# Windowed attention feeding a gated feed-forward layer: keys and queries brought straight into the score layout, head pairs scored together, partial first sums, and paced casts

## The chip, the cores and the metric

One core of one Trainium2 chip. The metric is the device time of one execution in microseconds (us); a profiled execution also has a span, the time between its first and last instruction, which lies about 1.7 us below the time. All inputs are fp32 in DRAM; the kernel computes in bf16 with fp32 sums.

## The reference, cut to what matters

```python
# q, k, v: (8 batches, 8 heads, 576 rows, 64)
scores = q @ k.transpose(0, 1, 3, 2) / sqrt(64)
rel = pos[:, None] - pos[None, :]
mask_plain = (rel >= 0) & (rel < 32)                       # heads 0-3
mask_dil   = (rel >= 0) & (rel < 128) & (rel % 4 == 0)     # heads 4-7
attn = softmax(where(mask, scores, -1e9)) @ v              # -> x: (4608, 512)
h = x @ w_in                                               # (512, 2048)
out = (h * sigmoid(beta * h)) @ w_out                      # (2048, 512)
```

Nearly all arithmetic is the two products: 9 tiles of 512 rows, each with 64 matmuls of 512 columns for `w_in` and 64 for `w_out`. The attention of batch b + 1 runs in between, as fill.

Of the kernel before, what the change touches and what calls it, by code (L numbers as in the profile page):

```python
# [22 lines left out]
class Op:  # L23
    def __init__(self, engs, fn, deps, vt, acquire, group, dma, lat):
        self.engs, self.fn, self.vt, self.acquire = engs, fn, vt, acquire
        self.deps = [d for d in deps if d is not None]
        self.dma, self.lat, self.group = dma, lat, group
        self.end = self.ready = None
        self.waits = 0
        self.next = []  # L30
        for g in group if isinstance(group, list) else [] if group is None else [group]:
            g.users.append(self)


class Plan:
# [3 lines left out]
    CAPS = {"h": 3, "o": 2, "z": 4, "a": 8, "s": 5}  # L39
# [6 lines left out]
    def op(self, engs, fn, deps=(), vt=0.0, acquire=None, group=None, dma=0, lat=None):  # L46
        acquire = acquire if acquire is None or isinstance(acquire, list) else [acquire]
        o = Op(engs, fn, deps, vt, acquire, group or acquire, dma, lat)
        self.ops.append(o)
        return o  # L50

    def run(self, filler=None, filler_until=0.0):
# [13 lines left out]
        ends = []  # L66

# [19 lines left out]
        while n_left:  # L87
            best = None
            near = {}
            for o in avail:  # L90
                base = o.ready
                at = {e: max([free[e], base] + [t for x, t in o.group.read.items() if x != e]
                             if o.group is not None and e != "PE" else [free[e], base]) for e, d in o.engs}
                fin = min(at[e] + d for e, d in o.engs)
# [18 lines left out]
            if filler is not None and s <= filler_until and free["PE"] + 300 < s:  # L113
# [5 lines left out]
                free["PE"] = now + 225  # L119
                continue  # L120
# [6 lines left out]
            o.fn(e)  # L127
            free[e] = s + d
            o.start, o.end = s, s + d + self.LAT[e]
# [27 lines left out]
FIRST = "KD0 QD0 KD1 QD1 KP0 QP0 KP1 QP1 S2 S3 T S00 S10 V20 V21 V30 V31 U V00 V10 X2 X3 X00 X10 S01 S11 V01 V11 X01 X11"  # L157
LATER = "S2 S3 T V20 V21 V30 V31 U S00 S10 S01 S11 X2 X3 V00 V10 X00 X10 S02 S12 V01 V11 X01 X11"
# [3 lines left out]
def kernel(  # L162
# [35 lines left out]
    ADDED = 1  # L198
    BY_DMA = 2
    SPLIT = 4  # L200
# [16 lines left out]
    def copy(e, out, in_):  # L217
# [10 lines left out]
    mask_e = {n: const([P, 2, 2, 2, QT // 2], BF16, f"maske_{n}") for n in ("FP", "PP")}  # L228
# [5 lines left out]
    warm = const([P, 1], FP32, "warm")  # L234

# [7 lines left out]
    ptt = const([P, 2, 288], BF16, "ptt")  # L243
    ptt_own = ptt[0:2 * KTL][:, :, 0:256].rearrange(
        "p c (h s) -> p c h s", h=4)[:, :, :, 0:2 * UT]
# [9 lines left out]
    raw = const([P, 2, 4, S // 2], BF16, "raw")  # L255
    vd16 = raw[:].rearrange("p z h m -> p (z h m)")[:, 0:1024].rearrange("p (h T d) -> p h T d", h=4, T=C)
    vd16_of = [vd16] * DIRECT + [st[b % 2][:, 0:1024].rearrange(
        "p (h T d) -> p h T d", h=4, T=C) for b in range(DIRECT, B)]
    kT = [const([P, WIN + S], BF16, f"kT{x}") for x in range(2)]
    kz = const([P, 4, WIN + S], BF16, "kz")  # L260
    qd = const([P, 4, 2, S // 2], BF16, "qd")
    qT = qd[:].rearrange("p (x f) e m -> p x (f e m)", x=2)[:, :, 0:S]
# [27 lines left out]
    def t_fill1(e):  # L290
        for x in range(2):
            nc.vector.memset(kT[x][:, 0:WIN], 0.0)
            nc.vector.memset(qt[x][:], 0.0)
# [60 lines left out]
    def t_late(e):  # L354
        band(mask_d[:], [[0, 4]], [(1, P)], 0, WIN - 1, 1.0, 0.0)
        for n in ("PP", "FP"):
            band(mask_e[n][:].rearrange("p a b e m -> p (a b) e m"), [[0, 4]], [(1, 2), (2, QT // 2)],
                 WIN, -1, 1.0, 0.0)
            band(mask_n[n][:].rearrange("p a b n -> p (a b) n"), [[0, 4]], [(1, QT)], WIN, -1, 1.0, 0.0)
        nc.gpsimd.memset(mask_e["FP"][0:WIN, 0], 0.0)  # L360
        nc.gpsimd.memset(mask_n["FP"][0:WIN, 0], 0.0)
        nc.gpsimd.memset(kz[:], 0.0)  # L362
    late_fill = plan.op([("POOL", 11500)], t_late, vt=-.3)


# [15 lines left out]
    def plain_v(b, p0, c0):  # L381
        return bass.AP(tensor=v.tensor, offset=v[b, 0].offset + (p0 - WIN) * D + c0 * QT * D,
                       ap=[[D, (P if not p0 else P - WIN) if not c0 else WIN], [QT * D, 4 * NI - c0], [1, D]])

    def direct_vp(b, deps, vt):
        if b:
            return [load("POOL", (vp[b % 2][:, :, 0:D], plain_v(b, 0, 0)), deps, vt, 768, .27, 1450,
                         1100 if b < DIRECT else 4000)]
        return [load("POOL", (vp[0][WIN:P, :, 0:D], plain_v(0, WIN, 0)), deps, vt, 576, .25),
                load("POOL", (vp[0][0:WIN, 1:, 0:D], plain_v(0, 0, 1)), deps, vt, 184, .25)]  # L390

    def direct_vd(b, deps, vt, tdeps=()):
        src = v[b, 4:8].rearrange("h (t T) d -> t h (T d)", T=C)[0:P]
        out = [load("POOL", (vd16_of[b].rearrange("p h T d -> p h (T d)"), src), deps, vt, 512, .35)]
        for c in range(2):
            src = bass.AP(tensor=v.tensor, offset=v[b, 4].offset + ((P - WIN) * C + c) * D,
                          ap=[[2 * D, 2 * KTL], [S * D, 4], [1, D]])
            out.append(load("POOL", (vt_[b % 2][:, c, :, 0:D], src), list(tdeps), vt + (.15 if b == 0 else .02 if b < DIRECT else 0) + .001 + .001 * c, 96, .2))
# [4 lines left out]
    def cast(b, z, deps, vt):  # L403
        dst = scratch[b, z] = dram_pool.tile([2, S * 4 * D], BF16, name=f"s{b}_{z}")
        src = (k, q)[z][b].rearrange("(x h) s d -> x (h s d)", x=2)
        return load("POOL", (dst[:].rearrange("x (a e) -> (x a) e", e=1024),
                             src.rearrange("x (a e) -> (x a) e", e=1024)), deps, vt, 1152, .38)

    def crossbar(b, z, h0, deps, vt):
        flat = scratch[b, z][h0 // 4]  # L410
        if h0:
            dst = (dk, dq)[z][b % 2][:].rearrange("p r h t -> p r (h t)")
            src = flat.rearrange("(a e) -> a e", e=C * D)
        else:
            dst = raw[:, z].rearrange("p h m -> p (h m)").unsqueeze(1)
            src = flat.rearrange("(a e) -> a e", e=P)
# [31 lines left out]
    xcopy = {}  # L448

    def back_dma(b, j, vt_of, vdone):  # L450

        rows = dram_pool.tile([S // 2, HD], BF16, name=f"x{b}_{j}")
        plain = rows[:, 0:HD // 2].rearrange("(i m e) c -> e m i c", e=2, m=QT // 2)
        out = []
        if b < DIRECT:
            out.append(plan.op(
                [("SP", 500)], lambda e: nc.sync.dma_start(
                    out=rows[:, 0:HD // 2].rearrange("(i m) c -> m i c", m=QT),
                    in_=xsp[j][:].rearrange("p a x h d -> p a (x h d)")),
                [vdone[0, j], vdone[1, j]], vt_of[f"X1{j}"], dma=1200, lat=2000))  # L460
        for e_ in range(2 if b >= DIRECT else 0):
            out.append(plan.op(
                [("SP", 500)], lambda e, e_=e_: nc.sync.dma_start(
                    out=plain[e_], in_=xsp[j][e_ * QT // 2:(e_ + 1) * QT // 2].rearrange("p a x h d -> p a (x h d)")),
                [vdone[0, j], vdone[1, j]], vt_of[f"X1{j}"], dma=600, lat=2000))
# [7 lines left out]
        if j:  # L473
            for c in range(C):
                dil.append(plan.op(
                    [("SP", 500)], lambda e, c=c: nc.sync.dma_start(
                        out=right[t1 - t0:, c], in_=xdt[(c % 2 * 2 + c // 2) * UT:(c % 2 * 2 + c // 2 + 1) * UT].rearrange("p x h d -> p (x h d)")),
                    [vdone["U"]], vt_of["X11"], dma=150, lat=2000))
# [13 lines left out]
        for x in range(4):  # L492
            xcopy[b, x, j] = o

    def attention(b, ld, names, vts):
# [4 lines left out]
        if b < DIRECT:  # L500
            for n in [x for x in names if x[0] in "KQ"]:
# [8 lines left out]
                def evac(e, g=g, z=z, kind=kind, i=i):  # L510
                    tp = bank(g, BF16)[:, 0:S]
                    if kind == "P":
                        dst = qT[:, i] if z else kT[i][:, WIN:]
# [4 lines left out]
                key = (("kT", "qT")[z], i) if kind == "P" else (("dk", "dq")[z], kv, i)  # L518
                steps[n] = [plan.op([dve(S), act(S)], evac, [tr, fill1] + war(key), vt, group=g)]
                wrote(key)  # L520
        else:
            vt = vt_of["zPRE"]
            ready = {"D": [ld["x", 0, 4], ld["x", 1, 4]]}
            ops = []
            for e_ in range(2):
                def spread(e, e_=e_):
                    rows = slice(64 * e_, 64 * e_ + 64)
                    dst = kz[rows, :, WIN:].rearrange("p h (m e) -> p h m e", e=2)[:, :, :, e_]
                    copy(e, dst, raw[rows, 0])
                o = plan.op([("POOL", 1200), ("DVE", 1400)], spread, [ld["x", 0, 0], late_fill] + war("kz"), vt)  # L530
                used(("raw", 0), o)
                ops.append(o)
            wrote("kz")
            w = war("qd", ("qT", 0), ("qT", 1))
            for e_ in range(2):
                for half in range(2):
                    def spread(e, e_=e_, half=half):
                        copy(e, qd[64 * half:64 * half + 64, :, e_], raw[64 * e_:64 * e_ + 64, 1])
                    o = plan.op([("DVE", 900)] + ([("POOL", 1150)] if half == e_ else []), spread,
                                [ld["x", 1, 0]] + w, vt)  # L540
                    used(("raw", 1), o)
                    ops.append(o)
            wrote("qd", ("qT", 0), ("qT", 1))
            ready["P"] = ops


        def mixed(e):
            copy(e, dkt[kv][:], dk[kv][:, :, :, CT - KTL:].rearrange("p r h k -> p h k r"))
        o = plan.op([("DVE", 450), ("POOL", 500)], mixed,
                    (steps["KD0"] + steps["KD1"] if b < DIRECT else ready["D"][0:1]) + war(("dkt", kv)), vt_of["T"] - .01)  # L550
# [4 lines left out]
        for c in range(2):  # L555
            def padded(e, c=c):
# [3 lines left out]
            o = plan.op([("DVE", 250), ("POOL", 300)], padded,  # L560
                        (steps["QD0"] + steps["QD1"] if b < DIRECT else ready["D"][1:]) + [fill1] + war(("qt", kv)),
                        vt_of["T"] - .01)
# [8 lines left out]
        vdeps["P"] = ld["vp"] + [(fill3, fill4)[kv]]  # L571
        def spread(e):
            copy(e, vd[kv][:, :, :, 0:D], vd16_of[b])
        o = plan.op([("POOL", 1100), ("DVE", 620)], spread,
                    [ld["vd"][0], (fill3, fill4)[kv]] + war(("vd", kv)), vt)
# [7 lines left out]
        def exp_and_mask(key, sop, g, vt, n, sc, w, m, tiles):  # L583
# [4 lines left out]
            if b >= ADDED or key == ("T",):  # L588
                def mask(e):
                    E[e].tensor_tensor(out=w(), in0=w(), in1=m(), op=ALU.mult)  # L590
                ex = plan.op([("POOL", 120 + 2.2 * n), ("DVE", 160 + .65 * n)], mask,
# [410 lines left out]
```

## The kernel before: the parts that the change and the argument touch

The kernel states operations with a wished position in the stream, and a planner of its own orders them on each engine at build time. So an edit of one wish moves other instructions as well. Four parts matter. From batch 3 on, K and Q of all eight heads are cast to bf16 in two DRAM-to-DRAM copies and transposed by the DMA crossbar (a DMA that transposes what it moves). Those of the dilated heads land in `dk` and `dq` ready for use; those of the plain heads land in `raw` and are spread by VectorE and GpSimd into full-height tiles padded with zero heads:

```python
# two casts per batch, released by the first gated tile of batch b - 2
cs = [cast(b, z, gop[b - 2, 0] + behind, b - 2 + .01 * z) for z in range(2)]
...
dst = kz[rows, :, WIN:].rearrange("p h (m e) -> p h m e", e=2)[:, :, :, e_]
copy(e, dst, raw[rows, 0])                      # spread of K, two copies per batch
...
copy(e, qd[64 * half:64 * half + 64, :, e_], raw[64 * e_:64 * e_ + 64, 1])   # Q, four
```

The plain scores of those batches then run over all 128 rows of the array, one head per matmul:

```python
nc.tensor.matmul(sc[:, a, h2 * QT:h2 * QT + QT],
                 lhsT=kz[:, 2 * x + h2, i * QT:i * QT + P],
                 rhs=qd[:, 2 * x + h2, :, i * QT // 2:(i + 1) * QT // 2], start=True, stop=True)
```

A first-product group waits for all of `xT` of its columns; the first four blocks of tile 0 are cut into column halves. The last block of the output is two halves of 256 columns, whose last half is evicted (copied from the accumulator banks to SBUF) in two pieces:

```python
for lo, hi in ((0, HD // 2), (HD // 2, HD)) if last_one else ((0, HD),):
    block_cols(t, tb, vts, lo, hi, (lo, (lo + hi) // 2, hi) if lo else (lo, hi))
```

The softmax here doesn't subtract the row's maximum and nothing guards it: scores larger than these inputs give would overflow.

## Time and profile before

| kernel before | |
|---|---|
| time, median of 3 | 311.83 us (311.3 to 311.83) |
| span of the profiled run, granted clock | 309.7 us, 0.998 |
| TensorE busy | 96% |
| first `w_in` product starts | 20.07 us |
| last product ends | 305.06 us |
| from there to the end | 4.65 us |

The granted clock is the share of the full TensorE clock that the chip allowed. The lines that bound the kernel are shown in the prediction.

### The profile page before, as it was taken

The page shows a single profiled execution, that of the slowest core. Times are in us where ns is not written, and L with a number is a line of the kernel's source. Part 1 is how long each engine was busy: PE and PEld are TensorE (multiplying, and loading weights), DVE is VectorE, ACT ScalarE, POOL GpSimd, SP SyncE. Part 2 cuts the span into 40 slices and gives each one's busy share as a digit, 9 for nine tenths or more (in the row PEclk, how much of TensorE's full clock was granted, in tenths as well). Part 3 has the DMA queues.
Part 4 walks back from the last instruction along what each step waited for, and adds up shares of the span by engine and source line. Part 5 has one row for each costly group of instructions (what it writes and reads, how often), then busy time and mean ns, then how long its engine had stood idle before and what let it go on. Part 6 is the DMA issues. An engine that isn't in the chain of part 4 may idle for free.

```text
span 309.7 us, 6029 instructions
## 1 busy us (share of the span) xinstructions
PE 297.0 (96%) x2270; PEld 153.6 (50%) x2307; DVE 199.1 (64%) x421; ACT 171.3 (55%) x302; POOL 108.6 (35%) x150
## 2 busy tenths in 40 slices
PE   7899999999999999999999999999999999999994
PEld 5565546454454445444455454445544444444452
DVE  4687868888958777775896878677853443434300
ACT  2668845866448445753775547555754544554311
POOL 8989754537170146414823651154000000000000
PEclk9999999999999999999999999999999999999999
DMA  6999999999689982999999759997024100001112
GB/s 100 168 210 207 206 187 208 230 155 174 155 163 178 191 151 83 180 160 181 188 206 181 197 117 177 129 224 163 18 64 112 44 34 34 36 34 60 42 70 69
DMA packets 93561, 42.48 MB, mean 137 GB/s; under 512 B 71052, under 2 KB 88220, under 8 KB 93212
## 3 DMA queue, kind: packets, MB, share of 16 engines
q0 software_dynamic: 42336, 19.66, 50.3%
q1 hardware_dynamic: 51052, 22.37, 35.0%
q8 instruction: 18, 0.29, 0.4%
q14 instruction: 11, 0.09, 0.1%
q10 hardware_dynamic: 144, 0.07, 0.1%
HBM read 39.32 MB, written 18.87 MB: 188 GB/s over the span
## 4 chain that ended last, share of the span: by engine, by line
PE 82%; POOL 6%; DMA 6%; DVE 2%; issue 2%; ACT 0%; POOLq 0%; ACTq 0%; DVEq 0%
PE bank L856 38%; PE bank L824 35%; DMA raw<-in_v_dram 3%; DMA vp<-in_v_dram 3%; PE bank L703 2%; PE bank L755 2%; POOL st L368 1%; PE bank L740 1%; PE bank L644 1%; PE bank L725 1%; POOL kz L362 1%; DVE qt L218 1%; DVE g L836 1%; PE bank L434 0%; PE bank L618 0%
## 5 line engine op out<-in xcount | busy, mean ns | idle before, releaser
L831 ACT ACTIVATE tnh<-bank,beta_half 128x512 bf16<-128x512 f32 (+2 forms) x148 | 100.1, 677 | 81.8 <-PE bank L824 73.6
L836 DVE SCALAR_TENSOR_TENSOR g<-tnh,bank 128x512 bf16<-128x512 bf16 (+2 forms) x148 | 98.7, 670 | 69.2 <-ACT tnh L831 68.1
L824 PE MATMUL bank<-xT,w_in_bf 128*128 128x512 bf16 (+2 forms) x576 | 139.8, 373 | 1.3 <-DVE xT L218 0.3
L856 PE MATMUL bank<-w_out_bf,g 128*128 128x512 bf16 (+1 forms) x571 | 137.7, 373 | 1.8 <-DVE g L836 0.5
L856 PEld LDWEIGHTS <-g 128*128 128x128 bf16 x592 | 55.4, 98 | 58.6 <-issue 0.8
L824 PEld LDWEIGHTS <-w_in_bf 128*128 128x128 bf16 x592 | 55.1, 98 | 58.2 <-issue 0.8
L873 ACT ACTIVATE osb<-bank 128x512 f32<-128x512 f32 (+2 forms) x36 | 21.0, 582 | 28.4 <-PE bank L856 23.5
L586 ACT ACTIVATE pt<-bank 128x384 bf16<-128x384 f32 (+1 forms) x54 | 22.0, 455 | 6.4 <-PE bank L703 3.5
L586 ACT ACTIVATE ptd<-bank 128x512 bf16<-128x512 f32 x32 | 17.0, 601 | 10.3 <-PE bank L644 10.3
L605 DVE TENSOR_TENSOR xsp<-bank,rcp 96x384 bf16<-96x384 f32 x32 | 17.7, 554 | 1.1
L604 DVE RECIPROCAL rcp<-bank 128x4 f32<-128x4 f32 (+2 forms) x72 | 12.8, 177 | 5.5 <-PE bank L755 2.8
L218 POOL COPY kz<-raw 64x1152 bf16<-64x1152 bf16 x6 | 9.4, 1566 | 18.4 <-DMA raw<-s 18.3
L218 POOL COPY vd<-st 128x1024 bf16<-128x1024 bf16 x4 | 4.1, 1037 | 30.9 <-DMA st<-in_v_dram 30.9
L590 DVE TENSOR_TENSOR ptd<-ptd,mask_d 128x512 bf16<-128x512 bf16 x24 | 13.0, 575 | 2.8 <-ACT ptd L586 2.5
L605 DVE TENSOR_TENSOR xdm<-bank,rcp 128x256 bf16<-128x256 f32 x32 | 13.6, 424 | 1.1
L590 POOL TENSOR_TENSOR pt<-pt,maske_FP 128x384 bf16<-128x384 bf16 x7 | 6.3, 912 | 20.4 <-ACT pt L586 12.4
L368 POOL DMA_DIRECT2D vp<-in_v_dram x9 | 12.0, 1338 | 2.6 <-DMA vp<-in_v_dram 2.6
L755 PEld LDWEIGHTS <-pt 128*128 128x128 bf16 x192 | 9.2, 97 | 6.5 <-DVE pt L590 0.6
L755 PE MATMUL bank<-vp,pt 128*128 128x65 bf16 x192 | 10.6, 193 | 0.9 <-DVE pt L590 0.5
L368 POOL DMA_DIRECT2D vt<-in_v_dram x16 | 11.0, 694 | 0.0
L875 DVE TENSOR_SCALAR osb<-bank 128x512 f32<-128x512 f32 (+1 forms) x2 | 1.0, 486 | 13.7 <-ACT osb L873 13.7
L218 DVE COPY qd<-raw 64x1152 bf16<-64x1152 bf16 x14 | 8.9, 634 | 0.9 <-DMA raw<-s 0.8
(125 smaller groups left out, 223.4 us busy)
## 6 DMA issues: line engine op xcount, KB each, us to landing
out_dram<-osb SPq DMA_DIRECT2D x35, 256.0 KB, 2.0
s<-in_k_dram POOLq DMA_DIRECT2D x5, 576.0 KB, 7.6
s<-in_q_dram POOLq DMA_DIRECT2D x5, 576.0 KB, 10.2
vp<-in_v_dram POOLq DMA_DIRECT2D x7, 384.0 KB, 14.8
w_out_bf<-in_moe_w_out_dram POOLq DMA_DIRECT2D x2, 1024.0 KB, 16.3
st<-in_k_dram POOLq DMA_DIRECT2D x6, 288.0 KB, 13.3
st<-in_q_dram POOLq DMA_DIRECT2D x6, 288.0 KB, 13.5
x<-xsp SPq DMA_DIRECT2D x20, 72.0 KB, 2.3
```

The lines of the kernel that those rows point to most:

```text
L218: (nc.scalar.copy if e == "ACT" else E[e].tensor_copy)(out=out, in_=in_)
L368: {"POOL": nc.gpsimd, "SP": nc.sync}[queue].dma_start(out=out, in_=in_)
L586: nc.scalar.activation(out=w(), in_=sc(), func=ACT.Exp, scale=SCALE)
L590: E[e].tensor_tensor(out=w(), in0=w(), in1=m(), op=ALU.mult)
L604: nc.vector.reciprocal(out=r, in_=p[..., D])
L605: nc.vector.tensor_tensor(out=dst, in0=p[..., 0:D], in1=r.unsqueeze(len(p.shape) - 1).to_broadcast(list(p.shape[:-1]) + [D]), op=ALU.mult)
L755: nc.tensor.matmul(pv[:, a, h2, :], lhsT=pt[x][:, (3 * j + a) * 2 + h2], rhs=vp[kv][:, (2 * x + h2) * NI + 3 * j + a, 0:D + 1], start=True ...
L824: nc.tensor.matmul(bank(g)[:, 0:n], lhsT=w_in_bf[:, kt, fb * P:(fb + 1) * P], rhs=xT[:, kt, xo:xo + n], start=(kt == 0), stop=(kt == NKT - 1))
L831: nc.scalar.activation(out=th[:, 0:n], in_=bank(g)[:, 0:n], func=ACT.Tanh, scale=beta_half[:, fb:fb + 1])
L836: nc.vector.scalar_tensor_tensor(out=g_t[t % 2][:, fb, c0:c0 + n], in0=th[:, 0:n], scalar=1.0, in1=bank(g)[:, 0:n], op0=ALU.add, op1=ALU.mult)
L856: nc.tensor.matmul(bank(g)[:, lo:hi], lhsT=g_t[t % 2][:, fb, tb * P:(tb + 1) * P], rhs=w_out_bf[:, fb, lo:hi], start=(fb == 0), stop=(fb = ...
L873: nc.scalar.mul(out=ob[:, cols], in_=bank(g)[:, cols], mul=0.5)
```

## The change

Its intent: shorten TensorE's attention stream, take layout copies off VectorE and GpSimd, start the dense part sooner, and release the loads of a later batch at a better moment. The core of the diff (the plumbing of tiles and dependencies is cut):

```diff
+        # one cast per four heads; the plain heads are put head-interleaved, 128-byte writes
+        if h0: args = (dst ... "(a e) -> a e", src "h s d -> (h s d)" ...)
+        else:  args = (dst[:].rearrange("(s h d) -> s h d", h=4, d=D), src.rearrange("h s d -> s h d"))
 ...
-            dst = raw[:, z].rearrange("p h m -> p (h m)").unsqueeze(1)      # and six spreading copies
+            dst = qT[kv][:] if z else kT[kv][:, :, WIN:]                    # crossbar to the score layout
 ...
+            if b >= PAIRED and x % 2:
+                continue
+            xs = (x, x + 1) if b >= PAIRED else (x,)                        # two head pairs per visit
 ...
-                            lhsT=kz[:, 2 * x + h2, ...], rhs=qd[:, 2 * x + h2, ...]
+                                bank(gs[2 * n + h])[:, a * QT:(a + 1) * QT], lhsT=kT[kv][rows, x, i * QT:i * QT + P],
+                                rhs=qT[kv][rows, x, i * QT:(i + 1) * QT], ...)   # rows: 64 of 128
 ...
-            cs = [cast(b, z, gop[b - 2, 0] + behind, b - 2 + .01 * z) for z in range(2)]
+            mid = (b - 2) * S + S // 2
+            def t_pace(e, b=b, mid=mid):
+                nc.gpsimd.tensor_copy(out=pace[:], in_=(
+                    xT[0:1, 0, mid - 1:mid + 1] if b - 2 >= BY_DMA else g_t[b % 2][0:1, 0, 0:2]))
+            go = plan.op([("POOL", 150)], t_pace, ..., b - 2.4)             # releases casts, vd, vp
 ...
+        parts = [((2, 3), 0, n), ((0, 1), 0, S // 2), ((0, 1), S // 2, n)] if apart else [((0, 1, 2, 3), 0, n)]
 ...
-        for lo, hi in ((0, HD // 2), (HD // 2, HD)) if last_one else ((0, HD),):
-            block_cols(t, tb, vts, lo, hi, (lo, (lo + hi) // 2, hi) if lo else (lo, hi))
+        cuts = (0, HD // 2, 3 * HD // 4, HD) if last_one else (0, HD)
+        for i, (lo, hi) in enumerate(zip(cuts, cuts[1:])):
+            block_cols(t, tb, [x + i for x in vts], lo, hi)
```

Three more parts of the diff: the mask fills of GpSimd move to the front; the tail group of batch 0 moves behind the start of the dense part; and the planner now keeps VectorE and GpSimd operations that are marked `sbuf` from running at the same time.

## The prediction

> **What bounds the kernel now.** I read the page first: busy time by engine, then the slices, then the waits of TensorE, and only then its instructions in order of time.
>
> ```profile
> span 309.7 us, 6029 instructions
> ...
> PE 297.0 (96%) x2270; PEld 153.6 (50%) x2307; DVE 199.1 (64%) x421; ACT 171.3 (55%) x302; POOL 108.6 (35%) x150
> ...
> PE   7899999999999999999999999999999999999994
> ...
> POOL 8989754537170146414823651154000000000000
> ...
> DMA  6999999999689982999999759997024100001112
> ```
>
> TensorE is busy in every slice but the first and the last; GpSimd has nothing left to do after about 220 us and DMA little. Busy is not yet bound, so the waits of TensorE come next (us in total, times, longest).
>
> ```profile
> PE bank L968 <- DVE warm L279: 1.1, 1, 1.1
> PE bank L740 <- DVE vd L218: 0.7, 1, 0.7
> PE bank L755 <- DVE pt L590: 0.5, 1, 0.5
> ```
>
> These are the longest; all fifteen together are 6.7 us, some of it before 20 us. So TensorE is bound by its own instruction stream, and a change helps only by shortening the stream, by starting the dense part sooner, or at the tail. How long an instruction holds the stream is read from start to start, not from its duration (512 columns last 379 ns but follow each other every 216):
>
> ```profile
> 110.32 3.62 PE L856 MATMUL bank<-w_out_bf,g 128*128 128x512 bf16 x16
> 113.87 0.62 PE L644 MATMUL bank<-dq,dk 64*128 64x128 bf16 x16
> 114.42 0.36 PE L618 MATMUL bank<-qt,dkt 128*96 128x64 bf16 x4
> ...
> 118.92 0.67 PE L703 MATMUL bank<-qd,kz 128*128 128x96 bf16 x12
> 119.43 1.03 PE L856 MATMUL bank<-w_out_bf,g 128*128 128x512 bf16 x3
> ```
>
> Full-height scores (L703, keys padded with zero heads): 12 in 0.51 us, 42.5 ns each, and no gap into the next kind. Half-height scores (L644, two heads side by side): 16 should take 8 x 56 = 0.45 us, but 0.55 us pass, and 16 x 215.8 = 3.45 us of L856 before them hold 3.55. So half-height pairs run at half price, and each change of array mode costs about 0.095 us, on the way in and out. The start:
>
> ```profile
> 19.31 0.49 PE L968 MATMUL bank<-zero 128*128 128x256 bf16 x3
> 20.07 1.14 PE L824 MATMUL bank<-xT,w_in_bf 128*128 128x288 bf16 x8 [0.27 <-DVE xT L218]
> ...
> 22.59 0.27 PE L968 MATMUL bank<-zero 128*128 128x256 bf16 x1
> 22.72 0.93 PE L824 MATMUL bank<-xT,w_in_bf 128*128 128x224 bf16 x8
> 23.83 4.39 PE L824 MATMUL bank<-xT,w_in_bf 128*128 128x224 bf16 x23 [0.18 <-DVE g L836]
> ```
>
> The first useful product waits for a copy into xT and begins at 20.07; its first four blocks (3.5 us of stream) are strung out over about 4.5 us, with fillers between. The tail, from the chain of waits:
>
> ```profile
> 305.31 0.29 ACT osb L873
> 305.60 0.02 issue
> 305.62 0.29 DVE osb L875
> ```
>
> The last two 128-column evictions were meant to run side by side and run one after the other.
>
> **What the Trainium skill says.** "TensorE: Matmul & The Clock Gate", section "Back-to-back issue gap", gives N/2.4 + 2.5 ns for a warm matmul: 215.8 ns for 512 columns, 42.5 for 96, and the trace agrees with both. The same section's sustained 131 ns for 512 columns is not what this trace shows. "TensorEngine Tiling (Array Packing)", section "Key Properties", says that changing the tiling mode drains the array; the 0.095 us above is that drain here. "DMA: Bandwidth & Descriptors", section "Specifications", wants at least 512 B per transfer for full rate; the V loads, 256-byte rows that become 128 bytes, take a median 14.8 us to land for 384 KB written, against 7.6 and 10.2 us for the 576 KB casts with long rows. That agrees, though queueing is in both.
>
> **The change part by part.** I counted matmuls and mode changes in the instruction order of both kernels and priced them with the rates above.
>
> (a) Plain scores from batch 3 on. Before: 5 batches x 24 x 42.5 ns = 5.1 us, no mode change. After: 5 x 12 pairs x 42.5 ns = 2.55 us. But the mode changes of the whole stream go from 73 to 85, 12 x 0.095 = +1.14 us; that already holds what pairing two head pairs per visit saves. (The dilated scores already stood 16 in a row before, as at 113.87, so pairing saves little there.) Net -1.4 us, all on the path.
>
> (b) Off the path: 30 spreading copies of K and Q vanish (from the rows by shape: DVE 14 x 0.634 + 4 x 0.982 = 12.8 us, GpSimd 6 x 1.566 + 6 x 1.207 = 16.6 us), and the zero fill of kz, about 2 us. Against them: eight exponentials of 288 columns per batch for six of 384 (columns equal, two more fixed costs, about 0.35 us of ACT per batch), and masks drifting from GpSimd to DVE. DVE is 64% and ACT 55% busy, so none of this is worth time by itself. It should relieve the waits on masks.
>
> (c) Start. First sums over the dilated heads (two of four K tiles) need only half of xT, and the plain V of batch 0 is loaded in halves, so products can begin before the plain heads are done. The limit becomes w_in: its first load was issued at 11.55 us and took 7.5, so 19.05. Two tail-V loads (1.35 us of GpSimd) move behind it and one V issue (about 0.9 us) is added; so it lands near 18.5. I put the first product at 18.6, and the four blocks (3.5 us) end near 22.5 instead of 24. The tail group of batch 0, its values and two small transposes (0.3 us of stream plus four mode changes, 0.7 us together) move behind the start, so they are repaid: net gain 0.9 us.
>
> (d) Later waits. Between 20 and 105 us I find gaps of about 2.3 us in the stream. The mask wait near 101.5 (0.5 to 0.7) and the vd waits near 40 (0.2 to 0.3 each) have causes the change touches: GpSimd was held by late mask fills from 19 to 30 us and by kz copies. I credit 0.7 us, and charge 0.4 us for new waits, since TensorE reaches batch 1 sooner while the same DMA stream must deliver it.
>
> (e) Tail. The last 256 columns become two groups of 128, each with one eviction: one eviction of 0.29 us leaves the chain; 16 extra matmuls cost 16 x 2.5 ns = 0.04. Net -0.25 us.
>
> Sum: -1.4 - 0.9 - 0.7 + 0.4 - 0.25 = -2.85 us; 311.83 becomes about 309.0.
>
> **The rivals.** First, DMA takes over. The plain-head casts now reorder rows as they go: 2304 rows of 256 bytes become 2304 writes of 128 bytes per tensor, where before a cast took 32 long packets. Ten such casts at some 2 to 3 us (estimated from a V load, 3072 such rows, of which the trace moves most within about 3 us once started) add about 2 us per batch. For it: DMA is at 9 in most slices up to 75 us. Against it: after 80 us a batch has some 31 us, with slices at 7, 5 and 0, and the finished attention lies about 60 us ahead of the end, where TensorE lives on products alone. A late batch 3 or 4 would show as one gap of 2 to 6 us; the time would be 311 to 315. I think batch 3 is rather helped, as its dilated casts now go first.
>
> Second, GpSimd becomes a gate: the pacing copy waits for landed xT columns in an in-order queue, and masks, V spreads and all loads behind it wait too. For it: in-order, and GpSimd already waits 30.9 us for V. Against it: scores of batch b come some 30 us of stream after the landing of b-2, and from batch 4 on all masks are on DVE in the new order. If it bites: 310 to 313.
>
> Third, the early gain is lost in the saturated start: DMA is full to about 66 us, batch 1's last Q load lands near 32.5 whatever TensorE does. Then (c) shrinks to 0.3 and the time is 309.6. Fourth, the opposite: nearly all gaps close and the start gains 2 us in full; then 306.8.
>
> **Range and chances.** The floor is hard: 1152 products of 512 columns at 215.8 ns are 248.6 us, and the attention stream falls by only 1.4. Over 2% faster means 305.6 or less, 6.2 us, more than twice my sum, so 7%. Over 2% slower means 318.1 or more; that needs DMA or GpSimd to stall TensorE for over 9 us net, 3%. Predicted 309.0 us; 8 in 10 between 306.4 and 311.6.
>
> **What would show it.** (a) Plain scores from batch 3 on as 64*128 matmuls, about 0.25 us per 12 and 0.095 us of gap on each side. (b) DVE and GpSimd busy time down together by roughly 10 to 15 us. (c) First w_in product near 18.6 us, four blocks done near 22.5. (d) No TensorE wait for pt above 0.3 us near 100. (e) A single 128-column eviction at the end. Wrong if the waits of TensorE name kT, qT or dk transposes, or if the start does not move: then the rival of DMA holds. If the span falls by much more than 3 us, I have mis-sized the gaps in the stream.

## The result, and the profile after

| | before | after |
|---|---|---|
| time, median (range) | 311.83 us (311.3 to 312.12) | 308.24 us (307.32 to 308.98) |
| ratio, 95% interval | | 0.9885 (0.985 to 0.9921) |

Here and below a ratio is the mean time of one kernel's runs over that of the other's runs of the same rounds, so not quite the ratio of the medians. Executions over 1.5% slower than the fastest of the same kernel are left out of the means. The change gains about 1.15%: surely a little faster. The page of the profile after:

```profile
span 305.6 us, 6034 instructions
...
PE 297.2 (97%) x2312; PEld 150.1 (49%) x2312; DVE 182.5 (60%) x420; ACT 171.0 (56%) x315; POOL 90.0 (29%) x132
...
DMA  6999999999799998999799999991333100010122
...
q0 software_dynamic: 65392, 19.66, 62.9%
```

TensorE is as full as before, VectorE (DVE) and GpSimd (POOL) together are 35 us less busy, and the DMA row has a 9 in nearly every slice up to the 27th, where before some of the later ones were a 2, 5 or 7: the queue that carries the casts moves the same 19.66 MB in 65,392 packets instead of 42,336. So the change trades compute copies for small DMA writes. The waits of TensorE (total, times, longest):

```profile
PE bank L637 <- DMA dq<-s: 1.4, 1, 1.4
PE bank L955 <- DVE warm L289: 1.1, 1, 1.1
```

The waits for a mask (pt) and for vd that the prediction showed are gone from the list. A new one of 1.4 us heads it: the dilated scores of batch 4 wait for their crossbar transpose. TensorE at the start, and where batch 4 is late:

```profile
18.75 1.02 PE L809 MATMUL bank<-xT,w_in_bf 128*128 128x512 bf16 x4
19.70 0.30 PE L778 MATMUL bank<-ident_b,xsp 96*128 96x96 bf16 x3
...
110.42 0.62 PE L637 MATMUL bank<-dq,dk 64*128 64x128 bf16 x16 [1.36 <-DMA dq<-s]
...
116.52 0.43 PE L671 MATMUL bank<-qT,kT 64*128 64x96 bf16 x12
```

The first product starts at 18.75 while batch 0's transposes (L778) are still under way: those are the partial sums. L671 is the new half-height visit: 12 matmuls follow within 0.36 us (116.52 to 116.88) including a mode change.

I summed each stream in one way: every TensorE instruction from the first `w_in` product on at its measured spacing (N/2.4 + 2.5 ns, half for half-height pairs, 0.095 us per mode change, which is a switch between full and part use of the array) gives the "priced stream"; what the products' real positions show beyond that is waiting. (The first trace of before lacks 37 matmul records, 2270 of 2307; its stream is that of the second, the same program.) Each kernel was profiled twice (the second profiles are the runs `e9_before_again` and `e12_after_again` below):

| us | before | before again | after | after again |
|---|---|---|---|---|
| first `w_in` product | 20.07 | 21.80 | 18.75 | 18.34 |
| priced stream | 279.59 | 279.59 | 279.01 | 279.01 |
| waits in it | 5.40 | 3.80 | 4.39 | 5.04 |
| last product ends | 305.06 | 305.19 | 302.15 | 302.39 |
| tail to the end of the span | 4.65 | 4.65 | 3.5 | 3.5 |

The rows of each column sum to the end of the last product (before, its start plus 216 ns x 256/512), and with the tail to the span. From before to after the stream gives 0.6, start and waits together (25.5 to 23.3 on average) 2.3, the tail 1.2. Only the sum of start and waits is worth reading: the two profiles of before start 1.73 us apart and end 0.13 apart. (In the second, a single run of unknown state, the granted clock was 0.82 from 15 to 20 us and 0.84 from 20 to 25, so part of its late start is the clock.)

**The tail.** The last evictions before and after, in order of time:

```profile
304.88 0.71 ACT L873 ACTIVATE osb<-bank 128x256 f32<-128x256 f32 x2 [1.15 <-PE bank L856]
305.29 0.99 SPq L881 DMA_DIRECT2D out_dram<-osb  x2
```

```profile
300.62 0.42 DVE L861 TENSOR_SCALAR osb<-bank 128x256 f32<-128x256 f32 x1 [11.62 <-PE bank L844]
...
302.35 0.29 DVE L861 TENSOR_SCALAR osb<-bank 128x128 f32<-128x128 f32 x1 [1.30 <-PE bank L844]
```

Before, the first 256 columns begin to be evicted at 304.88, only 0.18 us before the last product ends, because the products of both halves alternate. Their 128 KB store is issued at 305.29 and under way when the two 64 KB stores join it. After, the first half is evicted at 300.62 and long stored by then. The prediction looked at the last two evictions alone; the time at which the first half leaves is what it overlooked.

### The profile page after: what moved, and what is told of

Read it like the earlier page. It is cut to its first block, busy times and chain, and to the rows that moved or that the text cites. A ratio compares the mean times of both kernels' runs of the same rounds, so it can differ in the third digit from the quotient of the medians.

```text
span 305.6 us, 6034 instructions
## 1 busy us (share of the span) xinstructions
PE 297.2 (97%) x2312; PEld 150.1 (49%) x2312; DVE 182.5 (60%) x420; ACT 171.0 (56%) x315; POOL 90.0 (29%) x132
## 3 DMA queue, kind: packets, MB, share of 16 engines
q0 software_dynamic: 65392, 19.66, 62.9%
## 4 chain that ended last, share of the span: by engine, by line
PE 81%; DMA 11%; POOL 2%; DVE 1%; ACT 1%; issue 1%; SPq 1%; POOLq 0%; ACTq 0%; DVEq 0%
PE bank L809 36%; PE bank L844 36%; DMA st<-in_v_dram 4%; DMA dq<-s 3%; DMA st<-in_q_dram 3%; DMA x<-xsp 2%; PE bank L671 1%; PE bank L727 1%; PE bank L637 1%; DMA xT<-x 1%; PE bank L453 1%; PE bank L697 1%; PE bank L712 1%; PE bank L446 1%; POOL st L382 1%
## 5 line engine op out<-in xcount | busy, mean ns | idle before, releaser
L844 PE MATMUL bank<-w_out_bf,g 128*128 128x512 bf16 (+2 forms) x608 | 143.6, 368 | 0.0
L823 DVE SCALAR_TENSOR_TENSOR g<-tnh,bank 128x512 bf16<-128x512 bf16 x144 | 97.7, 685 | 73.8 <-ACT tnh L818 73.1
L809 PE MATMUL bank<-xT,w_in_bf 128*128 128x512 bf16 (+1 forms) x584 | 141.4, 376 | 0.0
L818 ACT ACTIVATE tnh<-bank,beta_half 128x512 bf16<-128x512 f32 x144 | 98.5, 689 | 75.2 <-PE bank L809 73.1
L859 ACT ACTIVATE osb<-bank 128x512 f32<-128x512 f32 (+1 forms) x36 | 21.2, 589 | 32.2 <-PE bank L844 32.1
L574 ACT ACTIVATE pt<-bank 128x288 bf16<-128x288 f32 x64 | 21.5, 419 | 5.7 <-PE bank L671 5.6
L382 POOL DMA_DIRECT2D vp<-in_v_dram x10 | 18.0, 1805 | 0.5 <-PE bank L453 0.5
L382 POOL DMA_DIRECT2D s<-in_q_dram x10 | 13.6, 1356 | 0.0
L382 POOL DMA_DIRECT2D s<-in_k_dram x10 | 11.0, 1103 | 1.2 <-issue 1.2
L578 DVE TENSOR_TENSOR pt<-pt,maskn_FP 128x288 bf16<-128x288 bf16 x27 | 7.9, 324 | 2.0 <-ACT pt L574 1.9
```

The lines of the kernel that those rows point to most:

```text
L382: {"POOL": nc.gpsimd, "SP": nc.sync}[queue].dma_start(out=out, in_=in_)
L574: nc.scalar.activation(out=w(), in_=sc(), func=ACT.Exp, scale=SCALE)
L578: E[e].tensor_tensor(out=w(), in0=w(), in1=m(), op=ALU.mult)
L809: nc.tensor.matmul(bank(g)[:, a:z], lhsT=w_in_bf[:, kt, fb * P:(fb + 1) * P], rhs=xT[:, kt, xo + a:xo + z], start=(i == 0 and kt == kts[0] ...
L818: nc.scalar.activation(out=th[:, 0:n], in_=bank(g)[:, 0:n], func=ACT.Tanh, scale=beta_half[:, fb:fb + 1])
L823: nc.vector.scalar_tensor_tensor(out=g_t[t % 2][:, fb, c0:c0 + n], in0=th[:, 0:n], scalar=1.0, in1=bank(g)[:, 0:n], op0=ALU.add, op1=ALU.mult)
```

## The experiments

Twelve kernels ran, all within the tolerance. Unless said otherwise each is the changed kernel with one edit. "Waits" are the gaps above 0.06 us between products after the first one, summed as above; the changed kernel has 2.4 us of them in its first profile and 3.1 in its second.

### e1_whole_sums: no partial first sums

```diff
-    APART = 4
+    APART = 0
```

> The changed kernel without partial first sums (APART 0): the first products wait for all of xT. If the start was won by the partial sums, the first product comes at 20 us or later instead of 18.75, the time is 1.0 to 1.6 us above the changed kernel's (about 309.5), and the rest of the stream is as before. If the start was won by loading V in halves and by deferring the tail group, the first product stays near 19 and the time within 0.5 us.

Measured: 308.02 us (307.98 to 308.43), ratio to before 0.9883 (0.9856 to 0.991). The first product starts at 20.51 instead of 18.75, yet the last one ends at 302.83, 0.4 to 0.7 us later than in the two profiles of the changed kernel. In the time nothing is seen. Where the lead of the changed kernel goes is seen by following one output eviction, the eighth, first in the changed kernel and then in this one. The last line shows the dilated scores of batch 4 in this one:

```profile
107.37 0.60 ACT L859 ACTIVATE osb<-bank 128x512 f32<-128x512 f32 x1 [0.18 <-PE bank L844]
```

```profile
109.48 0.60 ACT L859 ACTIVATE osb<-bank 128x512 f32<-128x512 f32 x1 [0.18 <-PE bank L844]
110.24 0.62 PE L637 MATMUL bank<-dq,dk 64*128 64x128 bf16 x16
```

The lead is still 2.1 us at 107 us, so the first tiles did not take it back. The changed kernel then waits 1.4 us before batch 4's dilated scores (110.42), and e1, which comes there later, does not wait; from 140 us on the evictions are 0.7 apart. A sooner start is worth little here because one later DMA chain does not come sooner with it: dq of batch 4 lands at 110.3 us there and at 108.6 here. The expectation was too high.

### e2_unpaired: half-height scores, one head pair per visit

```diff
-    PAIRED = 2
+    PAIRED = 8
```

> The changed kernel with one head pair per visit everywhere (PAIRED 8). Its instruction order has 109 mode changes in place of 85: at 0.095 us each +2.3 us on the dense part and on the time, if mode changes are a pure price on the stream. If they hide behind waits, less than 1 us; if smaller visits ease banks and evictions, the waits fall and part of it comes back.

Measured: 311.5 us (310.69 to 311.96), ratio 0.9987 (0.9962 to 1.0013): the whole gain is gone. The plan has 109 mode changes instead of 85. The dense part without its waits is 283.6 us instead of 281.0, so 24 more mode changes cost 2.6 us, 0.108 each, near the 0.095 that the prediction read; the remaining loss is waits (4.0 instead of 2.4 to 3.1). What it looks like, again from TensorE in order of time:

```profile
129.43 0.30 PE L671 MATMUL bank<-qT,kT 64*128 64x96 bf16 x6
130.63 0.30 PE L671 MATMUL bank<-qT,kT 64*128 64x96 bf16 x6
```

A visit of 12, as at 116.52 in the changed kernel, is split into two of 6, each with its own way in and out. Pairing is what makes half height affordable.

### e3_old_tail: the old evictions and stores, the new order of products

```diff
-        cuts = (0, HD // 2, 3 * HD // 4, HD) if last_one else (0, HD)
+        cuts = (0, HD // 2, HD) if last_one else (0, HD)
-            block_cols(t, tb, [x + i for x in vts], lo, hi)
+            block_cols(t, tb, [x + i for x in vts], lo, hi, (lo, (lo + hi) // 2, hi) if lo else (lo, hi))
```

The wish `x + i`, which keeps the halves apart, stays.

> The changed kernel with the old last block (256 columns, evicted in two parts by ScalarE and VectorE, stored from two queues). Theory of one eviction less: 0.3 us longer from the last product to the end. Theory that the second store queue itself is slow to finish: 1.0 us or more, as between the two first traces (4.65 against 3.45 us after the last product). If neither (0.1 us or less), those 1.2 us were chance of the two executions.

Measured: 307.34 us (306.62 to 307.83), ratio 0.9856 (0.9829 to 0.9882). The tail is 3.54 us, 0.1 above that of the changed kernel and 1.1 below that of before. So the one eviction fewer, which the prediction counted at 0.25, is worth 0.1; the other 1.1 of the tail is not in the evictions. In this run's trace the first half is evicted at 301.07, 1.5 us before the last product ends, as after.

### e4_full_height: paired visits over all 128 rows (wrong result)

```diff
-                            rows = slice(64 * h, 64 * h + 64)
+                            rows = slice(64 * h, 64 * h + 64) if b < DIRECT else slice(0, P)
```

The scores of two heads are added, which is wrong; with inputs this small the softmax is nearly even, and the result still passed the tolerance.

> Wrong result on purpose: from batch 3 on the plain scores are taken over all 128 rows (24 matmuls of 96 columns, 42.5 ns each, no mode change), with nothing else altered. Theory of the sum in the prediction: +2.55 us of matmuls, -20 mode changes of 0.095 us = -1.9, so the dense part grows by 0.65 us and the time by as much. If mode changes were free, +2.5 us; if half-height pairs were not at half price, less than 0.

Measured: 307.57 us (307.11 to 307.82), ratio 0.9863 (0.984 to 0.9887). Without its waits the dense part is 281.4 us against 281.0. Half height by itself, with its mode changes, is worth 0.4 us of stream (0.65 was expected) and nothing that the time shows.

### e5_gate_tie: casts released by the first gated tile of b - 2, as before

```diff
-                    xT[0:1, 0, mid - 1:mid + 1] if b - 2 >= BY_DMA else g_t[b % 2][0:1, 0, 0:2]))
+                    g_t[b % 2][0:1, 0, 0:2]))
-                xready(mid - 1, mid + 1) if b - 2 >= BY_DMA else gop[b - 2, 0]), b - 2.4)
+                gop[b - 2, 0]), b - 2)
```

> Casts of batch b released by the first gated product of tile b-2, as in the kernel before, in place of landed xT columns. If the tie to landed columns is what keeps the loads ahead, casts of batch 4 come later than 86 us and the gap before batch 4's dilated scores grows from 1.4 to 3 us or more; time +1 to +4 us. If the tie is only order, the time stays within 0.7 us.

Measured: 316.63 us (315.63 to 317.95), ratio 1.0157 (1.0117 to 1.0197), 8.4 us above the changed kernel. Waits of 10.5 us:

```profile
PE bank L637 <- DMA dq<-s: 2.8, 1, 2.8
PE bank L671 <- DVE g L823: 2.1, 1, 2.1
```

The pacing copies run at 94.2, 126.9, 157.6 and 183.9 us instead of 86.1, 116.4, 148.6 and 177.6. That is 6 to 11 us later, for every batch, and the scores wait for crossbars (dq) or for gate operations that were late themselves. This is the price of a late release in the new order of operations. It is not what the new release gained over the kernel before, which with the same tie issued its first casts of batches 4 to 7 at 87.4, 122.8, 149.8 and 182.4 us, at most 6 us behind the changed kernel's (86.6, 116.9, 149.1, 178.1). The edit also moves the wished place of the release (b - 2.4 to b - 2).

### e6_free_casts: casts released by the landed plain Q of b - 1

```diff
-                    xT[0:1, 0, mid - 1:mid + 1] if b - 2 >= BY_DMA else g_t[b % 2][0:1, 0, 0:2]))
+                    qT[(b - 1) % 2][0:1, 0, 0:2] if b > DIRECT else g_t[b % 2][0:1, 0, 0:2]))
-                xready(mid - 1, mid + 1) if b - 2 >= BY_DMA else gop[b - 2, 0]), b - 2.4)
+                [] if b > DIRECT else gop[b - 2, 0]), b - 2.4)
```

> Casts of batch b from 4 on released by the landed plain Q of b-1 (about 79 us for batch 4 in place of 86). If the 1.42 us gap at 108.7 comes from a release that is too late, it vanishes and the time falls by 1 to 1.4 us against the changed kernel. If the queue of SyncE (the back store and crossbar of batch 3 ahead of batch 4's) is the cause, the gap stays; if the earlier casts collide with batch 2's and 3's own transfers, a new gap shows before 100 us.

Measured: 314.32 us (313.98 to 314.39), ratio 1.0078 (1.006 to 1.0096). The release of batch 4 comes at 81.9 instead of 86.1. The wait at 109 is gone, and 8.9 us of others appear. A piece of the chain of waits (start, length), and VectorE in order of time there:

```profile
84.24 14.43 DMA st<-in_v_dram
```

```profile
98.76 0.43 DVE L232 COPY vd<-st 128x1024 bf16<-128x1024 bf16 x1 [6.07 <-DMA st<-in_v_dram]
99.11 1.88 DVE L823 SCALAR_TENSOR_TENSOR g<-tnh,bank 128x512 bf16<-128x512 bf16 x3
```

The loads of batch 4 now share the queues with the attention of batch 3 on its way back through DRAM. V takes 14.4 us to land, the copy that spreads it stands in VectorE's in-order stream and waits 6.07 us, and three gate operations that TensorE needs stand behind it. Too early costs time as well, by another way.

### e7_long_casts: the plain casts in long rows (wrong layout)

```diff
-            args = (dst[:].rearrange("(s h d) -> s h d", h=4, d=D), src.rearrange("h s d -> s h d"))
+            args = (dst[:].rearrange("(a e) -> a e", e=1024), src.rearrange("h s d -> (h s d)").rearrange("(a e) -> a e", e=1024))
```

> Wrong result on purpose: the plain-head casts keep the source order (16 long rows per tensor in place of 2304 short ones), planned as in the changed kernel, so every engine has the same order. If the short writes fill the queue and so delay batch 4's dilated crossbars, the 1.42 us gap of TensorE at 108.7 vanishes or falls below 0.5 and the time falls by 1 us or more. If the late release of the cast or the order of SyncE's queue is the cause, the gap stays at 1 us or more.

Measured: 308.12 us (306.66 to 308.95), ratio 0.9877 (0.9842 to 0.9913). The wait near 109 is gone, and by the semaphore records of the traces dq of batch 4 landed at 107.9 us instead of 110.3. But a wait of 1.3 us for a GpSimd mask appears at 72 us, so TensorE came to these scores only at 110.67, and the time is that of the changed kernel. That the 128-byte writes delay batch 4's crossbars is likely, and not shown: in e1, with the same writes, dq landed at 108.6. One gap was exchanged for another.

### e8_late_masks: the mask fills back to their old place

```diff
-    late_mask("D", 2600, ..., -7.215)
+    late_mask("D", 2600, ..., -.3)
-        late_mask("n" + n, 1900, t_mask_n, -7.183 + .001 * i)
+        late_mask("n" + n, 1900, t_mask_n, -.3 + .001 * i)
```

> Masks of batches 1 and later are filled after the early loads were issued, as late as in the kernel before (but without kz and the second mask shape). If the gaps around 40 and 47 us came from GpSimd held by mask fills, 0.3 to 0.8 us of waits return between 28 and 60 us; if they came from the saturated DMA stream, nothing changes (within 0.2 us of waits).

Measured: 307.82 us (307.34 to 309.85), ratio 0.9891 (0.9849 to 0.9933), the same gaps between 26 and 34 us as in the changed kernel's second profile. Early mask fills are worth nothing that can be seen.

### e9_before_again: the kernel before, unchanged

> The kernel before, unchanged, profiled once more. Question: is the tail of 4.65 us (span less end of the last product) of its first profile a property of its instructions or the luck of the last store's landing? Theory (luck): the tail is now 3.4 to 3.7 us, as in every other profile, the old tail restored in the new kernel included (3.54), and the span falls by about 1 us to 308.6 or so with the last product still ending near 305. Rival (property): again 4.4 to 4.9 us.

Measured: 311.54 us in its one run (310.28 to 312.85 over the eleven runs of the kernel before beside it). The tail is 4.65 us again, so the theory of luck falls: it is a property of the program. Two lines of the DMA view tell of a second part of it, here of the first profile, from 305.9 to 311 us in 40 slices:

```profile
GB/s 0 56 305 337 317 253 257 249 245 36 0 0 0 0 0 0 0 0 0 0 0 0 0 0 64 0 0 0 0 64 0 0 0 0 0 0 0 0 0 0
...
q14 instruction: 2, 0.02, 0.8%
```

The block on the left is the last stores; the two single slices of 64 GB/s after them are the two packets of an instruction queue in the second line, as nothing else moves there. Two such packets stand near the end in both profiles of before, none in those of the changed kernel (two of the experiments have one). Adding up, SyncE has seen the last store 3.42 us after the last product in both profiles of before, against 2.62 in that after: 0.8 us for the stores that leave together. Then GpSimd takes 0.40 us to answer SyncE in both, against 0.08 after: 0.3 us. What GpSimd waits for in these 0.40 us stays open: in the first profile the first of the two packets begins at 309.02, just after GpSimd has answered (308.99). No run undid `x + i` alone, so the 0.8 is read from the traces and not shown by an edit.

### e10_gate_tie_long: e5 and e7 together

The edits of e5_gate_tie and e7_long_casts in one kernel (wrong layout).

> The gate tie of the run before (casts of batch b released by g of b - 2, 316.6 us, 10.5 us of waits) together with the long, contiguous plain casts (wrong layout on purpose). Theory: it is the 128-byte writes that make the release time critical; with long packets the late release is nearly free: waits 4 us or less, time 308 to 311. Rival: the late release alone is what hurts (chain of cast, crossbar, scores, stores, transpose too long whatever the packets): waits 8 to 11 us, time 315 to 318.

Measured: 328.18 us (324.22 to 331.91, its slowest run not counted in the ratio), ratio 1.0488 (1.043 to 1.0546). The theory falls, and the rival's sizes too: waits of 23 us instead of 4, or 8 to 11. A piece of its chain of waits (start, length):

```profile
132.41 12.49 DMA dq<-s
```

Long packets do not help a late release: this is dq of batch 5, which took 12.5 us to land, against 11.1 and 11.7 for the same batch in the two profiles of the changed kernel. About 5 of the 23 us are a lower granted clock (0.979; 0.91 from 160 to 200 us): after each of its three longest waits products stand 427 instead of 216 ns apart for a while. Why it comes out worse than e5 beyond that stays open. Its pacing copies come 8, 8, 11 and 17 us after those of the changed kernel, in e5 8, 10, 9 and 6: here the lateness grows from batch to batch, in e5 it does not.

### e11_staged: dilated casts first, plain casts released by the landed dilated tiles

```diff
+                if n == 2 and b > DIRECT:
+                    ld[b]["vd"] = direct_vd(b, [go] + ...)
+                    def t_pace2(e, b=b):
+                        nc.gpsimd.tensor_copy(out=pace[:], in_=dq[b % 2][0:1, 0, 0, 0:2])
+                    go = plan.op([("POOL", 150)], t_pace2, [ld[b]["x", 0, 4], ld[b]["x", 1, 4]], b - 2.3)
```

> A candidate for a better version: from batch 4 on the dilated casts and loads go first and the plain casts (short writes) are released by a second pacing copy that waits for the landed dilated tiles. Theory: the gap of 1.4 us near 108.7 vanishes, nothing new, time 1 us below the changed kernel of the same rounds. Rival: the plain scores and values come too late, new gaps of 1 us or more name kT, qT or vp after 110, time equal to or above the changed kernel.

Measured: three runs of 308.28, 310.37 and 310.8 us and three slow ones of 316.05 to 317.21 (clock 0.988 to 0.989, left out). Ratio 0.9941 (0.9897 to 0.9984), against 0.9866 of the changed kernel in the same rounds. The wait of batch 4 is gone, as meant; the rival won. From its chain of waits, from 165 to 198 us:

```profile
172.82 9.69 DMA s<-in_q_dram
182.53 14.35 DMA qT<-s
```

The plain queries of a later batch were released at 171.2, and a cast of 9.7 and a crossbar of 14.4 us later TensorE had waited 2.4 us for them.

### e12_after_again: the changed kernel, unchanged

> The changed kernel, unchanged, in the rounds of the candidate, so that the two can be compared on one chip. Theory: 308.2 plus or minus 0.6 us, ratio to the kernel before 0.986 to 0.991, and in its profile again one wait of 1 to 1.5 us before the dilated scores of batch 4. Rival: the wait was the luck of one execution and is below 0.5 us.

Measured: 307.39 us (306.94 to 308.6), ratio 0.9866 (0.9837 to 0.9895). One wait of 1.35 us before the dilated scores of batch 4 again, so that wait belongs to the program.

## Why the prediction was right, point by point

The predicted 309.0 us came out as 308.24, and 307.39 in the later rounds: inside the range, and within 2% of before as thought most likely. The bound was read rightly: TensorE's own stream, which only stream, start or tail can move. The steps fared unevenly. (Two small slips in its sums: the fifteen waits are 6.3 us, not 6.7, and in (c) 1.5 less 0.7 is 0.8, not 0.9.)

**(a) Plain scores.** The priced stream fell by 0.58, as the terms of (a), the repaid 0.7 of (c) and the 0.04 of (e) add up to (-0.66). The price of a mode change is confirmed, not only assumed: 24 more cost 2.6 us in e2. "Pairing saves little there" was said of the dilated scores, and in e2 it holds: of the 13 visits that it has more, 11 are plain and 2 dilated. What (a) does not give is the cost of half height without pairing, which is as large as the whole gain (e2). Half height against full height in the new, paired plan is worth 0.4 (e4); pairing at full height in the kernel before was not run.

**(b) Off the path.** Too low in size: 16.6 us of VectorE and 18.7 of GpSimd went, 35 together instead of 10 to 15, and the copies and the fill that (b) itself lists come to 31. That it is worth no time by itself no run tested. The table of instruction groups by shape shows one reason besides the removed copies: mask products of 128 x 512 on VectorE last 449 ns on average instead of 575, and the copies into qt 189 instead of 492. The Trainium skill, "SBUF — State Buffer", section "SBUF: two separate sides", says that certain VectorE operations and GpSimd hold one pair of ports exclusively, so that the other "fully blocks". The change plans the marked operations of the two apart. These durations agree with that reading; no run isolates it.

**(c) Start.** The times were right: 18.75 for 18.6, and the four blocks done at 22.7 for 22.5 (before at 24.6, not 24). The worth was not. "Net gain 0.9" assumed that a sooner start moves the end by as much; in e1 only 0.4 to 0.7 of the 1.8 reaches the end. The third rival, "the early gain is lost in the saturated start", is not why: the lead over e1 outlives the saturated start and is 2.1 us at 107 us, and 1.4 of it is lost to the late batch 4, the first rival. The third rival is seen in the two profiles of before: of their 1.73 us, 1.1 are gone by 47 us, and the rest at 102 us, where the one that is ahead waits for a mask.

**(d) Later waits.** The size was near: start and waits together fell by 2.3, where (c) before its repayment and (d) add up to 1.9. Summed in the same way only up to 105 us, they fell by 3.6 to 4.0 against the second profile of before; the wait for batch 4 then takes 1.4 back. The cause named for it fell: early mask fills do nothing (e8). The mask wait near 101.5 did go, with the GpSimd and VectorE work around it. The new wait that was charged at 0.4 is one of 1.4, and it names a crossbar transpose (dq), as the prediction's sign of being wrong did for kT, qT or dk. What else closed the gaps was not isolated.

**(e) Tail.** This term was mis-sized: 0.25 predicted, 1.2 measured, and mostly by another cause. The dropped eviction is worth 0.1 (e3). As the traces read, about 0.8 is that the first half's store no longer leaves together with the last ones, and about 0.3 is GpSimd's late answer at the very end, whose cause stays open. Most of what the result is better than 309.0 lies here.

**The rivals.** The first, the DMA, was real in small form: one late batch, 1.4 us. Its chain, from the chain of waits after:

```profile
86.08 0.17 POOL pace L921
86.57 1.39 POOL s L382 x3
88.71 10.95 DMA st<-in_v_dram
...
102.09 8.19 DMA dq<-s
```

From the first cast of batch 4 at 86.6 to its scores, wanted at 109.0 and run at 110.4, there are 22 us, and it takes nearly 24. The kernel before had 26.5 (cast at 87.4, scores at 113.9). The second rival, the pacing copy as a gate, did not bite, but the new order depends on the place of its release: one 6 to 11 us later costs 8.4 us (e5), one 4 us sooner 6 (e6). The prediction treated it as a risk only and gave it no worth.

No version beat the changed kernel clearly. e3 and e12 are equal within their spread.

## What to carry to other kernels

Count array mode changes before tiles are halved: here a half-height form paid only with two pairs per visit. A release that paces loads has a narrow best place, since the chain of cast, crossbar and spread takes over 20 us and a late link sits in front of other work in an in-order engine, so try it on both sides. And look at the tail for when the first part of the last output leaves, not only at the last eviction; and follow an earlier start through the trace to where its lead is spent, since here 2.1 us of it lived to 107 us and 1.4 of that ended in one late DMA chain.

## What the Trainium skill lacked or had wrong

- "TensorEngine Tiling (Array Packing)", section "Key Properties", gives no figure for the drain of a mode change: 0.095 us read from before, 0.108 us each from 24 more of them in e2.
- "TensorE: Matmul & The Clock Gate", section "Back-to-back issue gap", holds 131 ns for sustained matmuls of 512 columns: here they stand 216 ns apart in every long run of them, in both kernels, with a weight load for each.
- "DMA: Bandwidth & Descriptors", section "DMA Transpose (X-bar)", has no latency under load: a crossbar of 288 KB took 8.2 us from issue to landing (dq of batch 4), 11.1 (dq of batch 5), 4.2 in e7, 12.5 in e10 and 14.4 in e11.
- "Runtime: NRT & Kernel Launch", section "Instruction fetch mechanics", says nothing of fetches at the end of a program: both profiles of before have two instruction packets after the last store, and there GpSimd's answer takes 0.40 us, against 0.08 in every other profile; whether one causes the other is open.
